# Attention and a mixture of experts on one core: the hand-written order of the attention's steps, all eight plans arranged anew

## Chip, cores and metric

One core of a Trainium2 chip runs the whole program. The metric is the device time of one execution in microseconds. The engines are named as in the profile: PE (TensorE), with PEld for its weight loads, ACT (ScalarE), DVE (VectorE), POOL (GpSimd) and SP (SyncE, which only issues DMAs here).

## What is computed

```python
def _attn_ref(q, k, v):                      # (8, 8, 576, 64), float32
    scores = scale * np.matmul(q, k.transpose(0, 1, 3, 2))
    mask = block_i >= block_j                # blocks of 64 positions
    scores = np.where(mask, scores, -1e9)
    scores = scores - np.max(scores, axis=-1, keepdims=True)
    attn = np.exp(scores)
    attn = attn / (np.sum(attn, axis=-1, keepdims=True) + 1e-09)
    return np.matmul(attn, v)
...
def _moe_ref(x, expert_emb, tau, w1, w2):    # x: 4608 rows of 512; 8 experts
    logits = xn @ en.T / tau                 # xn, en: rows divided by their norms
    expert_idx = np.argmax(logits, axis=1)
    gate_w = softmax(logits)[expert_idx]
    out[rows of e] = gate_w * (np.maximum(x @ w1[e], 0.0) @ w2[e])
```

## The kernel before

The 64 heads are worked off as 32 pairs (n = 0 to 31), four pairs to one of the 8 batches. Every pair goes through six kinds of work, each a Python generator that yields after every step. One letter of a plan string drives one generator by one step, so the string fixes the program order of all instructions, and with it the order in which each engine's queue gets them; each engine takes its queue strictly in order. In pair n the letters stand for:

- **s** (`scores`, 10 steps s1 to s10, five a head): scores of pair n, by a matmul over `ka`, `qb` (L400) and one over `kx`, `qx` (L401) into one of two PSUM tiles `pss`; then ACT takes the exp into `pT` (L410, L419), and POOL adds up `pT` into `pS` (L391).
- **v** (`values`, 9 steps): values of pair n-1. v1 to v6 multiply `pT` by `vo` (L435), where each head writes 64 columns of the array; v7 makes the sums over `pT` and `pS` with 32 columns each (L444, L445, L449); v8 is the copy of the result on ACT (L451); v9 is empty. All write the one PSUM tile `psb`.
- **f** (`post`, `finish`, 4 steps): pair n-1 is turned back. f1 and f2 are matmuls out of `so` into `psb` (L472, L476), f3 and f4 the divisions on DVE (L480 to L493).
- **m** (`maxes`, 12 steps): row maxima of pair n+1. m1 to m10 are a matmul into one of two PSUM tiles `psm` (L365) and a reduction on DVE (L367); m11 turns the maxima (L372), ACT copies them to `nmT` (L374), and two DMAs on SP's queue write them into a row of `qx` (L376), which the first score step of pair n+1 reads. m12 only ends the generator.
- **p** (`prep`, 6 steps): queries and keys of pair n+2. p1 transposes the queries on PE into the one PSUM tile `pst` (L322), ACT casts them (`qb`, L334); p2 casts `qd` (L338); p2 and p3 take the low parts on DVE (L311). p4 transposes the keys into `pst`, ACT casts `kd` (L343), SP issues four DMAs of `ka` (L346); p5 and p6 are the low parts.
- **r** (`slow[0]`): one step of the route of the batch before, if one is left: some 26 small DVE steps, a ranking on PE ("rk", L558 to L562), five squares and one exp on ACT, the store on SP, five scatters on POOL. The route of the seventh batch is followed by `early_rows`, which reads the table back by a DMA on SP (L649). An r without work does nothing.
- **w** and **l**: DMAs of `v` of pair n+3 on POOL's queue, and of `q`, `k` of pair n+3 on SP's.

```python
for c in PLANS[n % NP + (NP if n >= NPAIR - NP else 0)] if n else PLAN0:
    ...
    elif c != "r":
        parts[c] = drain(parts[c], 1)
    if c == "r" and slow and drain(slow[0], 1) is None:
        slow.pop(0)
```

Pair 0 has its own plan, plan n % 4 serves pairs 1 to 27 (plan 0 for six of them, plans 1 to 3 for seven each), and plans 4 to 7 the last four pairs. Pair 30 has no p left, pair 31 neither m nor p. After the pairs come the last values and finish, the slots' table, and the experts' layers (L1046), which the change doesn't touch.

Of the kernel before, what the change touches and what calls it, by code (L numbers as in the profile page):

```python
# [18 lines left out]


PLANS = (
    "rrrrlrvrvvvrvrrvrrrrsmmvvvmrrrmrrrrssprrrmrrrrrsrrmfprmmsrrrrrrrrsprrfrrmmsrsrmmffrrrrrrrrrprprrrsrprrrrrrrrswrrr",
    "vvvvrvvmmssvvmvmsspmsmpfmmsplfmsmspfmsmswfrpp",
    "mrmvvvrvvvvlrvmvpmssmwpfmrmsrpsfmrmssprmsfsrmfsrppms",
    "rrmmrvvlvvrvvvrrrvvmrmssrpwrmrssmpfmmrssfpmmfrssmpfsrrrmsrpprrr",
    "lvvvvmmpsrmsrrrrmvvpprrrvvrrrssrrrrvmmrppsrrsrrmrfrmrsrrpsrrrrmmffsfrmsrwm",
    "mrrmlpvvrvvrvprpvrmmrssrprmsmvsvrmvrsrrsmfmrrfrrrrmrfrswsmsmfrrprsrrrp",
    "prmmvvvrrvrvvrmssrpmrrrrrrrvvrsrmsmvrssrmmfmmfrrrsrlrfrsprprfwrprmrmsrps",
    "vvvmmrvmssvmmrvmmrpmrrssvsrvsmvrsrsrppmlfrfssmppmrfwpf",
)  # L30
PLAN0 = "kmsmsmmsmmkpsmsspkmmmpmslwsspspp"

# [1392 lines left out]
```

## Time and profile before

| | |
|---|---|
| median of three runs | 867.48 us (866.99 to 870.44) |
| profiled execution | 867.11 us |
| its span, first to last instruction | 865.4 us |
| mean granted clock of TensorE | 0.987 |
| busy: PE, PEld, DVE, ACT, POOL | 839.7, 676.4, 585.2, 491.4, 593.4 us |
| pairs 0 to 31 end at about | 410 us of the span |

Busy times are unions of the instructions' spans; matmuls are pipelined and overlap, so a busy PE need not be a PE at its peak. In the timelines below, rows stand in order of start, equal instructions that follow each other are merged with their count, and the distance between the starts of two rows is the time for which the first one kept PE from the second.

### The profile page before, as it was taken

The numbers are of one execution on the slowest core, as the hardware profiler recorded it, in microseconds if no ns is written. First come the engines' busy times: TensorE is split into PE (matmuls) and PEld (weight loads), VectorE is DVE, ScalarE is ACT, GpSimd is POOL, SyncE is SP. The second block draws the span as 40 slices with busy tenths as digits, with TensorE's granted clock in tenths as the row PEclk, the third lists the DMA queues.
The fourth block names the chain that finished last, engine by engine and source line by source line (L and its number), as shares of the span: only waits on it lengthen the run. The fifth ranks groups of instructions, "written<-read, shape, count | busy, mean of one in ns | idle before, by whom it ended". The sixth has DMA issues, their size and how long they took to land. (4 is left out here: it accounts for less than half of the span.)

```text
span 865.4 us, 19039 instructions
## 1 busy us (share of the span) xinstructions
PE 839.7 (97%) x5148; PEld 676.4 (78%) x5148; DVE 585.2 (68%) x1275; ACT 491.4 (57%) x959; POOL 593.4 (69%) x756
## 2 busy tenths in 40 slices
PE   8999999999999999998899999999999999999996
PEld 4777787777877788776678888888888888888874
DVE  8567887888888897883885634755766544665541
ACT  4556786868776776875745544654645333553321
POOL 6466787887778787688444444656677787777871
PEclk8799999999999999999999999999999999999998
DMA  7787887778788878884547434646777444444441
GB/s 151 175 186 145 173 179 171 167 167 174 168 182 173 171 178 177 191 202 148 160 128 276 142 133 148 220 166 209 237 247 238 156 154 149 140 144 148 152 121 34
DMA packets 141532, 146.69 MB, mean 170 GB/s; under 512 B 98889, under 2 KB 108329, under 8 KB 139852
## 3 DMA queue, kind: packets, MB, share of 16 engines
q1 hardware_dynamic: 115868, 91.58, 43.2%
q0 software_dynamic: 18896, 41.45, 16.6%
q10 hardware_dynamic: 6624, 12.06, 3.8%
q8 instruction: 51, 0.84, 0.4%
q14 instruction: 93, 0.76, 0.3%
HBM read 85.12 MB, written 31.79 MB: 135 GB/s over the span
## 5 line engine op out<-in xcount | busy, mean ns | idle before, releaser
L367 DVE TENSOR_REDUCE nmx<-psm 128x1 f32<-128x320 f32 x315 | 135.6, 453 | 54.0 <-PE psm L365 49.0
L410 ACT ACTIVATE pT<-pss 128x448 f32<-128x448 f32 (+1 forms) x254 | 108.1, 449 | 60.0 <-PE pss L401 57.7
L391 POOL TENSOR_TENSOR pS<-pS,pT 128x320 f32<-128x320 f32 x189 | 112.3, 594 | 17.4 <-ACT pT L410 2.7
L400 PE MATMUL pss<-qb,ka 128*128 128x448 f32 (+1 forms) x382 | 117.7, 322 | 3.4 <-ACT pT L410 1.4
L1046 PE MATMUL py<-ring_h,hh 128*128 (+1 forms) x288 | 112.7, 391 | 0.5 <-issue 0.5
L401 PE MATMUL pss<-qx,kx 70*128 70x448 f32 (+1 forms) x382 | 108.5, 311 | 4.9 <-DMA qx<-nmT 3.7
L1046 PE MATMUL py<-ring_h,hl 128*128 (+1 forms) x288 | 112.2, 390 | 0.0
L1046 PE MATMUL py<-ring_l,hh 128*128 (+1 forms) x288 | 112.1, 389 | 0.0
L391 POOL TENSOR_TENSOR pS<-pT 128x448 f32<-128x448 f32 x63 | 71.9, 1141 | 58.0 <-ACT pT L410 57.2
L1046 PE MATMUL ph<-ring_h,xh 128*128 x280 | 110.0, 393 | 0.0
L1046 PE MATMUL ph<-ring_h,xl 128*128 x280 | 109.3, 390 | 0.0
L1046 PE MATMUL ph<-ring_l,xh 128*128 x280 | 109.2, 390 | 0.0
L365 PE MATMUL psm<-kd,qd 128*128 128x320 f32 x315 | 98.3, 365 | 0.8 <-DVE nmx L367 0.4
L435 PE MATMUL psb<-pT,vo 128*64 128x448 f32 (+4 forms) x768 | 95.4, 397 | 1.2 <-issue 1.1
L812 DVE TENSOR_TENSOR ring_l<-raw,ring_h 128x1024 f32 (+1 forms) x64 | 83.0, 1308 | 19.1 <-ACT ring_h L808 14.3
L400 PEld LDWEIGHTS pss<-qb,ka 128*128 128x128 f32 x382 | 73.3, 192 | 18.2 <-ACT pT L410 11.1
L1064 ACT ACTIVATE h<-ph 128x512 f32<-128x512 f32 x70 | 41.7, 597 | 79.3 <-PE ph L1046 65.5
L435 PEld LDWEIGHTS psb<-pT,vo 128*64 128x64 f32 x768 | 50.6, 138 | 43.4 <-issue 32.8
L401 PEld LDWEIGHTS pss<-qx,kx 70*128 70x128 f32 x382 | 73.5, 193 | 7.3 <-DMA qx<-nmT 3.3
L973 POOL DMA_INDIRECT xg<-xbuf,rowq x64 | 64.9, 1014 | 20.4 <-issue 18.9
L973 POOL DMA_INDIRECT ex<-xbuf,rowq x64 | 63.4, 991 | 20.0 <-issue 17.1
L808 ACT CAST ring_h<-raw 128x1024 f32 (+1 forms) x68 | 70.3, 1053 | 6.8 <-ACTq L955 4.1
(278 smaller groups left out, 1815.5 us busy)
## 6 DMA issues: line engine op xcount, KB each, us to landing
raw<-in_moe_w_dram SPq DMA_DIRECT2D x40, 512.0 KB
ka<-kd SPq DMA_DIRECT2D x128, 144.0 KB
raw<-in_moe_w_dram SPq DMA_DIRECT2D x12, 1024.0 KB
hrows<-h ACTq DMA_DIRECT2D x46, 256.0 KB
hq<-hrows POOLq DMA_DIRECT2D x92, 128.0 KB, 3.1
qn<-in_q_dram SPq DMA_DIRECT2D x64, 144.0 KB
kn<-in_k_dram SPq DMA_DIRECT2D x64, 144.0 KB
qx<-qb SPq DMA_DIRECT2D x32, 288.0 KB
```

What stands on the lines that cost most here:

```text
L365: nc.tensor.matmul(mx[:, 0:max(e - a, 256)], qd[d][:, j, :, :], kd[d][:, a:a + max(e - a, 256)], start=True, stop=True)
L367: nc.vector.tensor_reduce(m[:, j + u:j + u + 1], mx[:, 0:e - a], axis=AX.X, op=ALU.max, negate=True)
L391: eng.tensor_tensor(o, pT[0:r, P:S] if t == 1 else o, pT[0:r, off[t]:off[t] + w], op=ALU.add)
L400: nc.tensor.matmul(o, ka[i][:, hh, ts], qb[i][:, hh, c0:c1], start=True, stop=False)
L401: nc.tensor.matmul(o, kx[i][0:KX, hh, ts], qx[i][0:KX, hh, c0:c1], start=False, stop=True)
L410: nc.scalar.activation(pT[:, o:o + c1 - c0], st[:, 0:c1 - c0], AF.Exp, scale=scale)
L435: nc.tensor.matmul(ob[hh * D:(hh + 1) * D, c0:c1], a[:, t, hh, :], pTs[hh][0][:, o:o + c1 - c0], start=(t == 0), stop=(c0 == OB or t == NJ ...
L808: return nc.scalar.copy(piece(ring_h, to, c, half), raw[i][:, c * CW:(c + 1) * CW])
L812: return eng.tensor_tensor(piece(ring_l, to, c, half), raw[i][:, c * CW:(c + 1) * CW], piece(ring_h, to, c, half).bitcast(F32), op=ALU.sub ...
L973: nc.gpsimd.indirect_dma_start(out=to, out_offset=None, in_=src, in_offset=bass.IndirectOffsetOnAxis(ap=at, axis=0))
L1046: m = nc.tensor.matmul(out, a[:, c, :], w, start=(c == 0 and w is wh and a is sh), stop=(c == nk - 1 and a is sl_))
L1064: nc.scalar.activation(h[:, f:f + 512], ph, AF.Relu)
```

## The change

The eight strings of `PLANS` are replaced; `PLAN0` and all else stay. The numbers of s, v, f, m and p steps are the same in each plan, r varies. In plans 0 to 3 v1 to v6 stand in two groups (with v7 apart from them: three) where they were one, and m steps often stand two together, between scores.

```diff
 PLANS = (
-    "rrrrlrvrvvvrvrrvrrrrsmmvvvmrrrmrrrrssprrrmrrrrrsrrmfprmmsrrrrrrrrsprrfrrmmsrsrmmffrrrrrrrrrprprrrsrprrrrrrrrswrrr",
-    "vvvvrvvmmssvvmvmsspmsmpfmmsplfmsmspfmsmswfrpp",
-    "mrmvvvrvvvvlrvmvpmssmwpfmrmsrpsfmrmssprmsfsrmfsrppms",
-    "rrmmrvvlvvrvvvrrrvvmrmssrpwrmrssmpfmmrssfpmmfrssmpfsrrrmsrpprrr",
-    "lvvvvmmpsrmsrrrrmvvpprrrvvrrrssrrrrvmmrppsrrsrrmrfrmrsrrpsrrrrmmffsfrmsrwm",
-    "mrrmlpvvrvvrvprpvrmmrssrprmsmvsvrmvrsrrsmfmrrfrrrrmrfrswsmsmfrrprsrrrp",
-    "prmmvvvrrvrvvrmssrpmrrrrrrrvvrsrmsmvrssrmmfmmfrrrsrlrfrsprprfwrprmrmsrps",
-    "vvvmmrvmssvmmrvmmrpmrrssvsrvsmvrsrsrppmlfrfssmppmrfwpf",
+    "vvrrvmrmprrrssmrmvvvmwrrrsrrmrsrlrrvrrmvsrrrsprrrrrmmrrprfmrffrrrsrfrsmprprrsrrrpmsvr",
+    "vrlvvvmssmmsmsrpmmrvrvvmmvsspmpfmfswsmfpfrpsvspm",
+    "vrvrvrvmsmpmsmvvvvswsplpmmfmffsspmmsfsmvrrrrrppsmmrs",
+    "rmrvrvrrrvvrmmpmvvrrmsrrsrvvmmsrlspmrrrfrrrrpmrrsrrrsrmrrrfssfmpsfpmrrrsvrrwp",
+    "rrmrmvvrrplrrrrmrsrrrrmvrvvrppvwvrvvmrsmrprrrmrsprrsrrmrprrfrrmrssrmfsfrrrmsrrfmsrsr",
+    "rrrmpmvvrsrlrrrsmrrrrpsvvvvrrrvrmrrrvrsmsmrrfpwmrsmrrpmrmrfssfmfmrpsrvrpsr",
+    "rmmvprrprrrlvrvrvrrvvvmvrsmsmrrpsprrsmmrfrprmsrmspmfrsffsmwrmsrsv",
+    "prvrvrmvrmvmmrmpssrvrvrrrmrrrssprvmvrlsrsrrsrrmmmrmrsrrrrfrpfrprfrrwsvpfrsm",
 )
 PLAN0 = "kmsmsmmsmmkpsmsspkmmmpmslwsspspp"
```

## Rows read from the trace of the kernel before

**Rows 1.** Profile page, part 1: busy time, share of the span, instructions.
```profile
PE 839.7 (97%) x5148; PEld 676.4 (78%) x5148; DVE 585.2 (68%) x1275; ACT 491.4 (57%) x959; POOL 593.4 (69%) x756
```

**Rows 2.** Stretches: length, busy (count) of PE, PEld, DVE, ACT, POOL; clock; DMA.
```profile
157.50:205.70 48.20, 47.76 (x396) 38.32 (x396) 40.47 (x116) 35.83 (x81) 38.22 (x51) 1.00 0.81 174
```

**Rows 3.** PE's timeline, plan 1: start, length, instruction, count.
```profile
177.49 0.28 PE L400 MATMUL pss<-qb,ka 128*128 128x256 f32 x1
177.61 0.29 PE L401 MATMUL pss<-qx,kx 70*128 70x256 f32 x1
...
177.97 2.92 PE L435 MATMUL psb<-pT,vo 128*64 128x128 f32 x24
180.82 0.53 PE L365 MATMUL psm<-kd,qd 128*128 128x320 f32 x2
181.19 0.30 PE L400 MATMUL pss<-qb,ka 128*128 128x288 f32 x1
```

**Rows 4.** PE's timeline, around score steps in plans 3 and 2.
```profile
162.83 0.66 PE L472 MATMUL psb<-idx,so 128*128 128x144 f32 x4
163.23 0.49 PE L365 MATMUL psm<-kd,qd 128*128 128x256 f32 x2
163.82 0.40 PE L400 MATMUL pss<-qb,ka 128*128 128x288 f32 x1
...
198.02 0.49 PE L365 MATMUL psm<-kd,qd 128*128 128x256 f32 x2
198.71 0.39 PE L400 MATMUL pss<-qb,ka 128*128 128x256 f32 x1 [0.20 <-ACT pT L410]
```

**Rows 5.** PE's timeline, three places in plans 2, 5 and 7.
```profile
146.21 0.29 PE L400 MATMUL pss<-qb,ka 128*128 128x288 f32 x1
147.17 0.40 PE L401 MATMUL pss<-qx,kx 70*128 70x288 f32 x1 [0.67 <-DMA qx<-nmT]
...
376.68 0.30 PE L401 MATMUL pss<-qx,kx 70*128 70x288 f32 x1
378.01 0.69 PE L322 MATMUL pst<-ident,kn 96*128 96x96 f32 x6 [1.03 <-issue]
...
400.52 0.40 PE L400 MATMUL pss<-qb,ka 128*128 128x288 f32 x1
402.26 0.40 PE L401 MATMUL pss<-qx,kx 70*128 70x288 f32 x1 [1.35 <-DMA qx<-nmT]
```

**Rows 6.** SP's timeline before the first and last of these places.
```profile
141.14 3.11 SPq L346 DMA_DIRECT2D ka<-kd  x4
144.35 1.56 SPq L376 DMA_DIRECT2D qx<-nmT  x2
...
399.98 0.34 SPq L649 DMA_DIRECT2D et<-table  x1
400.41 1.58 SPq L376 DMA_DIRECT2D qx<-nmT  x2
```

**Rows 7.** PE's timeline in plan 4, where the products stand in two groups.
```profile
358.75 2.48 PE L435 MATMUL psb<-pT,vo 128*64 128x128 f32 x16
361.16 0.53 PE L365 MATMUL psm<-kd,qd 128*128 128x320 f32 x2
...
363.56 0.37 PE L365 MATMUL psm<-kd,qd 128*128 128x448 f32 x1
363.86 0.66 PE L435 MATMUL psb<-pT,vo 128*64 128x192 f32 x8
364.45 0.30 PE L444 MATMUL psb<-pT,ones 128*32 128x128 f32 x1
```

**Rows 8.** ACT's groups by form, 157.5 to 205.7: busy, mean ns; idle before.
```profile
L338 ACT CAST qd<-qb 64x576 fp32r<-64x576 f32 x8 | 5.3, 666 | 0.1
```

**Rows 9.** DVE's timeline, first and last row of step f3, plan 3.
```profile
356.89 0.15 DVE L480 TENSOR_SCALAR rin<-psb 128x2 f32<-128x2 f32 x1
...
357.94 0.20 DVE L493 TENSOR_TENSOR lgh<-psb,rin 128x48 f32<-128x48 f32 x1
```

## The prediction

> **What bounds the kernel now.** I read the page first, then busy time by stretches, then the timeline of TensorE (PE) from start to start, and last the timelines of SP and VectorE (DVE) at the places where PE stood still. The page has PE busy 97% of the span [rows 1], but a matmul's row reaches past the start of the next one, so rows overlap and "busy" hides what a matmul costs. The distance between two starts is what counts below.
>
> The attention part repeats exactly every four pairs, since plans 0 to 3 take turns; I call that a round. A round takes 48.2 us, and in it DVE is busy 40.5 us, ScalarE (ACT) 35.8, GpSimd (POOL) 38.2 and PE 47.8, at a granted clock of 1.00 [rows 2]. So PE sets the pace, DVE has 16% to spare, and an order can win only what PE loses by waiting or by changing its mode.
>
> What one matmul takes: 0.12 us for 256 columns (177.49 to 177.61) [rows 3], so I price others by their columns, 0.21 us for 448, 0.27 us for 320 and 256 together, 0.13 us for 288.
>
> What PE waits for. (a) Score steps: two pss buffers, so step s waits for the exp of the second step before it. From 163.23 two matmuls of 256 (0.24 us) reach to 163.82: 0.35 us lost; from 198.02 the same work reaches to 198.71: 0.45 us lost [rows 4]. A round has four such places of 0.33 to 0.45 us and two or three smaller ones, 2.0 us together. (b) The first score step of a pair needs the maxima's row, brought by two DMAs on SP: at 146.21 PE goes on only at 147.17, 0.83 us late [rows 5]. SP had four ka transfers to issue first, 3.11 us from 141.14, and the nmT ones came behind them at 144.35 [rows 6]. That is at the first scores of plan 2, and plan 1 has p4 (which issues ka) before the maxima's last step m11. It occurs in three rounds, 2.6 us together. (c) In the last round: p4 waits from 376.68 to 378.01 for its one pst buffer, 1.2 us late, and the first score of the last pair from 400.52 to 402.26, 1.6 us late [rows 5], because SP sat in the route's table read (L649, at 399.98) before it could issue nmT at 400.41 [rows 6].
>
> **The change, part by part.** No instruction is added or removed: the same steps in another order on each queue.
>
> *Mode changes.* The values' products (v1 to v6) use 64-column tiles, their sums (v7) 32-column tiles, all else the whole array. Plans 0 to 3 had v1 to v6 in one stretch. That stretch takes 2.85 us (177.97 to 180.82), and the two matmuls behind it 0.37 us instead of 0.27, as the first load of weights lies open [rows 3]. Old plan 4 already splits them: v1 to v4 take 2.41 us and v5, v6 0.59 us, 0.15 us more than in one piece, and the matmul of 448 columns ahead of the second stretch holds PE 0.30 us instead of 0.21 [rows 7]. So one more visit to the tiles costs 0.15 + 0.09 + 0.10 = about 0.35 us, half of it for each change of mode. Counted from the strings (PE steps alone, r, w and l left out), the changes of mode rise by 2 in plan 0 (runs 6 times), 1 in plan 1, 2 in plan 2 and 3 in plan 3 (7 times each): 12 + 42 = 54. Plans 4 and 7 keep theirs, plan 5 has one more, plan 6 one fewer. 54 x 0.175 = **+9.5 us**. No cover hides it: PE is the engine that sets the pace. Below: if a change of mode falls into time in which PE would wait anyway, it costs nothing; above, 0.45 us a visit, 12 us.
>
> What the load behind a stretch shows is open time, 0.10 us. The Trainium skill's TensorE: Matmul & The Clock Gate (its opening table, queue depth) has TensorE pull weight loads ahead of matmuls in flight; by that the 0.10 would go and the sum would be 27 x 0.25 = 6.8 us. Its TensorEngine Tiling (Array Packing), Key Properties, says that changing the tiling mode drains the engine, which would leave 9.5 us. The trace sides with the second.
>
> *Score steps against ACT.* The casts of qd (two of 0.67 us [rows 8]) and the copy of so stand in ACT's queue near the middle of each pair, and the waits (a) lie behind them. Between s6 and s7, old plan 0 gives PE f2, m9, m10: 0.40 us for the four matmuls of f2 (162.83 to 163.23) [rows 4] and 0.24, so 0.64. The new one has m8, m9, f1, m10, f2 there: with f1 at some 0.8 (six such matmuls and three small transposes, by the same row) about 1.6. In plan 1 the work before s7 grows alike, in plan 2 that before s5 (m5, m6, f1, m7, f2 where f2, m8, m9 stood). Three of the four large waits should go, with the load left open behind each: about 1.1 us a round. In plan 3 only m10 and f2 stand between s6 and s7, so that one stays.
>
> *DVE's queue.* What comes in their place. (i) f3 and f4 free the one psb buffer that v1 of the next plan needs. f3 is DVE work from 356.89 to 358.14, 1.25 us [rows 9]. New plans 1 and 3 put f3 next to m11, and plans 2 and 0, which follow them, begin with v1; in the old order plan 2 began with two maxima, and plan 3 had f3 ahead of s7. (ii) New plan 3 has the route's exp (ACT) and the two steps that read it in the middle of the pair, next to each other, where the old order had p5 and p6 between: DVE then stands until ACT has got through the qd casts, and m9, m10, f3 and f4 wait behind it, on PE m11 and v1. Neither wait shows in the trace of before, so I bound the two: nothing, if DVE's 16% covers them, and at most ACT's two casts plus f3, 2.6 us a round. I take 0.8, nearer to the bottom, as the route's other work is as long as before. Net with the 1.1 above: -0.3 us a round, 6.75 rounds, **-2.0 us**; bounds -13 (all 2.0 us go, nothing comes) and +10.
>
> *SP's queue.* In new plans 0, 1 and 3 m11 stands ahead of p4, so nmT no longer queues behind ka; in plan 2 the next scores come 5 us later. PE has v1 to v4, m1 and more between m11 and the first score, about 4 us. Wait (b) goes: **-2.6 us** (bound 0, if the shorter way to s1 uncovers it elsewhere).
>
> *Last round.* The table read moves from behind f2 of plan 6 to before its s3, well ahead of m11, so SP is free for nmT: -1.6. p4 of plan 5 moves far behind p1: -1.2. But plan 5 has the route's ranking on PE (rk) directly behind m3, after eight DVE steps that begin with the plan; PE reaches it after about 2.8 us, DVE after 3 to 4: +0.8. **-2.0 us**; bounds -6 (all waits of these four pairs) and +2. The last pair has neither m nor p, and its order on PE is as before.
>
> GpSimd and the clock: plan 0's loads of v (w) now stand directly behind v6, which delays the adds of this pair, but the sums that need them come a pair later; PE stays busy, so I expect 1.00 throughout.
>
> Sum: 9.5 - 2.0 - 2.6 - 2.0 = +2.9 us. The profiled execution took 867.11 us, 0.4 below the median of 867.48 and 1.7 above its own span; 867.1 + 2.9 = **870.0 us**.
>
> **Rivals.**
> 1. The waits go and nothing takes their place (faster). For it: the stretches of v gave ACT nothing to do for 2.9 us at a time, and with scores between them ACT and DVE are fed evenly. The 1.4 us of mode changes a round also gives both more time. Against it: f3, f4 late in plans 1 and 3. Then -1.8 us a round, -12, with 9.5 - 2.6 - 3: **859 us**. It decides from about 1.7 us a round of waits removed.
> 2. DVE's queue takes over (slower): the exp of plan 3 and f4 before v1 hold PE 2.3 us a round where I took 0.8. Then 9.5 + 8 - 2.6 - 1: about **881 us**. For it: DVE is at 84% already. Against it: it idles at the start of most pairs. It decides from about 1.2 us a round.
> 3. The order does nothing: visits to the tiles fall where PE would wait anyway, and waits only change places: 867 us. It is part of "within 0.5%".
>
> **Numbers.** Differences under 0.5%, 4.3 us, can hardly be told from none here. The forecast with rival 3 gets 0.40, rival 1 0.26, rival 2 0.34. Faster is rival 1: 0.26; slower is rival 2 with the upper edge of the forecast, 0.38; within, 0.36. The range from 859 to 884 leaves out the far ends of both rivals.
>
> **What would show it.** A round in the new trace: 48.2 + 1.4 - 0.3 = about 49.3 us by the forecast, under 48 by rival 1, over 50.5 by rival 2. Two stretches of L435 a pair, three of L435 and L444 in plan 3, with 0.37 us behind each. No gap at the first L401 of plan 2 in the early rounds, nor near 402 us. By rival 2, L435 or L372 starts late behind DVE in plans 0, 2 and 3. The forecast is wrong if a visit costs much less than 0.35 us, or if ACT's waits return at other steps.

## The result and the profile after

The changed kernel takes 876.6 us (median of seven runs, 875.4 to 877.7), the kernel before 867.48 (seven runs beside them): a ratio of 1.0087, 95% interval 1.006 to 1.0115. The profiled execution is the slowest of the seven (877.7); it has a span of 876.0 us, 10.6 more than before, at a mean granted clock of 0.989.

Part 1 of the page, and a steady round of four pairs, cut from the last score of pair 16 to that of pair 20:

```profile
PE 846.6 (97%) x5148; PEld 672.1 (77%) x5148; DVE 603.6 (69%) x1275; ACT 489.0 (56%) x959; POOL 598.3 (68%) x756
```
```profile
230.73:280.56 49.83, 48.74 (x394) 37.64 (x392) 42.65 (x117) 35.30 (x80) 38.53 (x52) 1.00 0.76 169
```

The counts on the page are those of [rows 1]. The round takes 49.83 us where it took 48.2 [rows 2], at a clock of 1.00 in both. DVE is busy 2.2 us longer in it with the same work.

A pair's length is the distance between the starts of the last L401 of 64 columns of two successive pairs. In us, pairs 17 to 20, by the plan that orders them:

| kernel | plan 1 | plan 2 | plan 3 | plan 0 | four pairs |
|---|---|---|---|---|---|
| before | 11.82 | 12.68 | 11.75 | 11.93 | 48.18 |
| after | 12.28 | 12.62 | 12.88 | 12.05 | 49.83 |
| e1_split | 12.17 | 13.17 | 12.20 | 12.19 | 49.73 |
| e2_join | 11.96 | 12.32 | 12.90 | 12.70 | 49.88 |
| e5_route3 | 17.75 | 12.63 | 12.05 | 12.29 | 54.72 |
| e8_m11first | 12.01 | 12.75 | 11.77 | 11.92 | 48.45 |

Up to the end of pair 27 the new kernel is 9.8 us behind (368.3 against 358.5). The last four pairs give back 2.0 (417.8 against 410.0). From there to the end of the span it needs 2.8 more (458.2 against 455.4): 9.8 - 2.0 + 2.8 = 10.6. Two of these three hold a part that belongs to the execution and not to the order. In the last four pairs a stretch at half clock (0.50 granted) took 1.6 back (pair 29 below). And the 2.8 are 4.2 more in the seam, as I call the time from the last score to the 200th of the experts' products (70.1 against 65.9), and 1.4 less behind the last product (7.3 against 8.7), where executions with the old last strings differ as much: 7.0 in e3_new0to3, 9.4 in e6_et.

**Two visits to the tiles.** PE's timeline in pair 13 (plan 1):

```profile
180.66 2.48 PE L435 MATMUL psb<-pT,vo 128*64 128x128 f32 x16
183.07 0.42 PE L365 MATMUL psm<-kd,qd 128*128 128x320 f32 x1
183.33 0.29 PE L400 MATMUL pss<-qb,ka 128*128 128x288 f32 x1
...
186.78 0.41 PE L365 MATMUL psm<-kd,qd 128*128 128x320 f32 x1 [0.27 <-DVE nmx L367]
187.12 0.66 PE L435 MATMUL psb<-pT,vo 128*64 128x192 f32 x8
187.71 0.30 PE L444 MATMUL psb<-pT,ones 128*32 128x128 f32 x1
```

2.41 and 0.59 us are what plan 4 of the kernel before showed for the two groups [rows 7]. The maxima's matmul ahead of the second group waits for DVE.

**Who is waited for.** PE's loads of weights, waits by cause from 100 to 420 us; first the kernel before, then after:

```profile
PEld pss L400 <- ACT pT L410: 10.0, 30, 0.8
PEld psm L365 <- DVE nmx L367: 2.3, 7, 0.4
```
```profile
PEld pss L400 <- ACT pT L410: 2.8, 9, 0.4
PEld psm L372 <- DVE nmx L367: 6.2, 6, 1.0
PEld psm L365 <- DVE nmx L367: 5.2, 16, 0.5
```

The score waits of [rows 4] are mostly gone, and waits for the maxima have come: 7.2 us less of the one, 9.1 more of the other. The six at L372 are step m11 of plan 3, one a round. PE, DVE and ACT around the one in pair 19:

```profile
267.28 0.28 PE L372 MATMUL psm<-ident,nmx 128*9 128x128 f32 x1 [0.65 <-DVE nmx L367]
...
265.35 0.20 DVE L611 TENSOR_REDUCE gs<-lg 128x5 f32<-128x40 f32 x1 [0.84 <-ACT lg L609]
...
266.01 0.76 DVE L311 TENSOR_TENSOR qb<-pst,qb 64x576 fp32r<-64x576 f32 x1
266.80 0.42 DVE L367 TENSOR_REDUCE nmx<-psm 128x1 f32<-128x128 f32 x2
...
263.70 1.36 ACT L338 CAST qd<-qb 64x576 fp32r<-64x576 f32 x2
265.08 0.24 ACT L609 ACTIVATE lg<-lg 128x40 f32<-128x40 f32 x1
```

ACT comes to the route's exp (L609) behind its two qd casts, DVE stands 0.84 us in front of L611, and behind L611 in its queue are two more route steps, p3's low part and the last two maxima. Those end past 267, and m11 with them.

**Pair 29** got longer (15.98 us against 14.69), and that is the clock of this execution. In it the granted clock is at 0.50, its lower level (1.2 GHz), for 3.4 us; before had none between 33.6 us and the kernel's last 6. e9_lock_after and e2_join have the same strings for the last four pairs and ran pair 29 at full clock; and with the strings of before pair 29 met the lower level too, in e1_split and e8_m11first:

| execution | strings of the last four pairs | at half clock in pair 29 | pair 29 | the four pairs |
|---|---|---|---|---|
| before | old | none | 14.69 | 51.5 |
| e9_lock_after, e2_join | new | none | 14.36, 14.37 | 47.9, 47.9 |
| e1_split, e8_m11first | old | 3.4 us | 16.19, 16.09 | 52.9, 52.9 |
| after | new | 3.4 us | 15.98 | 49.5 |

So at like clock the new strings win 3.4 to 3.5 us in the four pairs, and pair 29 is 0.1 to 0.3 us shorter. It is so although the ranking waits for DVE (1.06 us here, 0.78 in e9), and a small comparison of DVE takes six times its usual 0.20 us, for as long as POOL's addition beside it runs. PE, DVE and POOL after, then the stretch at half clock, and the whole pair in e9 (columns as in [rows 2]):

```profile
385.53 0.18 PE L558 MATMUL psm<-ohb,triS 128*128 128x40 bf16 x1 [1.06 <-DVE ohb L550]
384.12 1.23 DVE L548 TENSOR_TENSOR ohb<-t,mx 128x40 bf16<-128x40 f32 x1
384.17 1.13 POOL L391 TENSOR_TENSOR pS<-pT 128x448 f32<-128x448 f32 x1
```
```profile
385.80:389.20 3.40, 3.40 (x11) 1.28 (x12) 2.02 (x7) 2.08 (x6) 2.49 (x4) 0.50 0.99 324
```
```profile
379.57:393.93 14.36, 13.16 (x106) 9.71 (x105) 12.70 (x42) 11.13 (x28) 10.49 (x16) 1.00 0.74 204
```

**Pair 31** is 2.2 us shorter. Its first scores run without the wait of [rows 5], since SP had issued nmT by 399.1:

```profile
397.56 1.55 SPq L376 DMA_DIRECT2D qx<-nmT  x2
...
401.20 0.30 PE L400 MATMUL pss<-qb,ka 128*128 128x288 f32 x1
401.33 0.30 PE L401 MATMUL pss<-qx,kx 70*128 70x288 f32 x1
```

**Behind the pairs** DVE splits the experts' first weights (L812) and turns the low part of their inputs (`xl`, L1039), on which PE waits. Ahead of that it makes four of the last pair's additions (L391). DVE and POOL in the kernel before:

```profile
411.23 1.00 DVE L391 TENSOR_TENSOR pS<-pT 128x448 f32<-128x448 f32 x1
413.93 2.36 DVE L812 TENSOR_TENSOR ring_l<-raw,ring_h 128x1024 fp32r<-128x1024 f32 x2 [0.18 <-ACT xh L1038]
416.21 0.68 DVE L1039 TENSOR_TENSOR xl<-pe,xh 128x512 fp32r<-128x512 f32 x1
416.81 7.31 DVE L812 TENSOR_TENSOR ring_l<-raw,ring_h 128x1024 fp32r<-128x1024 f32 x3
...
415.88 2.69 POOL L812 TENSOR_TENSOR ring_l<-raw,ring_h 128x1024 fp32r<-128x1024 f32 x1 [2.67 <-ACT ring_h L808]
420.24 6.11 POOL L812 TENSOR_TENSOR ring_l<-raw,ring_h 128x1024 fp32r<-128x1024 f32 x2 [1.67 <-ACT ring_h L808]
```

and after, with PE's two waits:

```profile
419.07 1.95 DVE L391 TENSOR_TENSOR pS<-pT 128x448 f32<-128x448 f32 x1
423.27 4.53 DVE L812 TENSOR_TENSOR ring_l<-raw,ring_h 128x1024 fp32r<-128x1024 f32 x2 [0.25 <-issue]
427.72 0.68 DVE L1039 TENSOR_TENSOR xl<-pe,xh 128x512 fp32r<-128x512 f32 x1
428.32 7.81 DVE L812 TENSOR_TENSOR ring_l<-raw,ring_h 128x1024 fp32r<-128x1024 f32 x3
...
423.71 3.01 POOL L812 TENSOR_TENSOR ring_l<-raw,ring_h 128x1024 fp32r<-128x1024 f32 x1 [0.77 <-ACT ring_h L808]
...
428.46 0.50 PE L1046 MATMUL pss<-ring_h,xl 128*128 128x512 f32 x1 [3.23 <-DVE xl L1039]
437.25 0.50 PE L1046 MATMUL pss<-ring_h,xl 128*128 128x512 f32 x1 [1.47 <-DVE xl L1039]
```

POOL's piece begins 5.9 us behind the last score in both kernels. DVE comes later: POOL's gathers and additions of the last pair end 5.1 us behind that score (3.2 before), DVE's four additions beside them take 3.7 us (2.3 before), and its first subtraction starts 1.5 us later. Its first two subtractions then take 4.53 us instead of 2.36: before, POOL's piece began when they were nearly done; now POOL begins 0.44 us behind DVE's start, and DVE's second one waits it out. In the kernel before only the second of PE's waits is there, 0.92 us. In e2_join, with the same last strings, POOL's piece came 0.8 us later, DVE's two took 2.36, and the seam is 67.4 us, 1.5 over before's.

### The profile page after: what moved, and what is told of

Read it like the earlier page. It is cut to its first block, busy times and chain, and to the rows that moved or that the text cites. A ratio compares the mean times of both kernels' runs of the same rounds, so it can differ in the third digit from the quotient of the medians.

```text
span 876.0 us, 19023 instructions
## 1 busy us (share of the span) xinstructions
PE 846.6 (97%) x5148; PEld 672.1 (77%) x5148; DVE 603.6 (69%) x1275; ACT 489.0 (56%) x959; POOL 598.3 (68%) x756
## 5 line engine op out<-in xcount | busy, mean ns | idle before, releaser
L410 ACT ACTIVATE pT<-pss 128x448 f32<-128x448 f32 (+1 forms) x254 | 109.2, 451 | 68.6 <-PE pss L401 61.7
L391 POOL TENSOR_TENSOR pS<-pS,pT 128x320 f32<-128x320 f32 x189 | 112.6, 596 | 23.6 <-ACT pT L410 6.6
L391 POOL TENSOR_TENSOR pS<-pT 128x448 f32<-128x448 f32 x63 | 72.4, 1150 | 68.8 <-ACT pT L410 68.6
L400 PE MATMUL pss<-qb,ka 128*128 128x448 f32 (+1 forms) x382 | 118.2, 325 | 0.5 <-ACT pT L419 0.4
L401 PE MATMUL pss<-qx,kx 70*128 70x448 f32 (+1 forms) x382 | 108.4, 310 | 3.1 <-DMA qx<-nmT 2.9
L365 PE MATMUL psm<-kd,qd 128*128 128x320 f32 x315 | 104.3, 365 | 2.2 <-DVE nmx L367 1.9
L435 PE MATMUL psb<-pT,vo 128*64 128x448 f32 (+4 forms) x768 | 103.2, 405 | 1.8 <-issue 1.1
L812 DVE TENSOR_TENSOR ring_l<-raw,ring_h 128x1024 f32 (+1 forms) x64 | 85.6, 1349 | 19.1 <-ACT ring_h L808 13.9
L435 PEld LDWEIGHTS psb<-pT,vo 128*64 128x64 f32 x768 | 48.7, 139 | 42.7 <-issue 36.9
L365 PEld LDWEIGHTS psm<-kd,qd 128*128 128x128 f32 x315 | 56.4, 191 | 31.7 <-issue 17.8
L400 PEld LDWEIGHTS pss<-qb,ka 128*128 128x128 f32 x382 | 73.6, 193 | 8.5 <-ACT pT L410 3.4
L401 PEld LDWEIGHTS pss<-qx,kx 70*128 70x128 f32 x382 | 73.7, 193 | 5.1 <-DMA table<-zcol 2.6
```

Of the source, the lines that this page charges most:

```text
L365: nc.tensor.matmul(mx[:, 0:max(e - a, 256)], qd[d][:, j, :, :], kd[d][:, a:a + max(e - a, 256)], start=True, stop=True)
L391: eng.tensor_tensor(o, pT[0:r, P:S] if t == 1 else o, pT[0:r, off[t]:off[t] + w], op=ALU.add)
L400: nc.tensor.matmul(o, ka[i][:, hh, ts], qb[i][:, hh, c0:c1], start=True, stop=False)
L401: nc.tensor.matmul(o, kx[i][0:KX, hh, ts], qx[i][0:KX, hh, c0:c1], start=False, stop=True)
L410: nc.scalar.activation(pT[:, o:o + c1 - c0], st[:, 0:c1 - c0], AF.Exp, scale=scale)
L435: nc.tensor.matmul(ob[hh * D:(hh + 1) * D, c0:c1], a[:, t, hh, :], pTs[hh][0][:, o:o + c1 - c0], start=(t == 0), stop=(c0 == OB or t == NJ ...
```

## The experiments

All were timed beside the kernel before: e1 to e4, e5 to e8 and e9 to e12 went together, with medians of 867.2, 866.9 and 869.5 for it. Ratios are to it, with 95% intervals.

### e1_split: the second visit to the tiles alone

The plans of before, with one PE step (s or m) moved between v4 and v5 in plans 0 to 3, so that the changes of mode rise by 54:

```diff
-    "vvvvrvvmmssvvmvmsspmsmpfmmsplfmsmspfmsmswfrpp",
+    "vvvvrmvvmssvvmvmsspmsmpfmmsplfmsmspfmsmswfrpp",
...
-    "rrmmrvvlvvrvvvrrrvvmrmssrpwrmrssmpfmmrssfpmmfrssmpfsrrrmsrpprrr",
+    "rrmmrvvlvvrmvvvrrrvvrmssrpwrmrssmpfmmrssfpmmfrssmpfsrrrmsrpprrr",
```

> The order of before; in plans 0 to 3 alone, v5 and v6 move behind the next score or maxima step, so that every pair of these plans visits the 64-column tiles twice (54 changes of mode more, as many as the change adds). Theory A, each change of mode costs PE 0.175 us: +9.5 us, about 877 us, and a round of 49.6 us where before has 48.2. Rival B, the visits fall into time in which PE would wait anyway: within 2 us of before.

876.8 us, ratio 1.0104 (1.0065 to 1.0143). The four pairs of the table grow by 0.35, 0.49, 0.45 and 0.26: 1.55 us for four added visits, 0.39 each, with whatever else the moved step did. This edit alone makes the kernel as slow as the whole change.

### e2_join: the change without the second visit

The new plans with v1 to v6 in one stretch in plans 0 to 3 (40 changes of mode fewer):

```diff
-    "vrlvvvmssmmsmsrpmmrvrvvmmvsspmpfmfswsmfpfrpsvspm",
+    "vrlvvvvvmssmmsmsrpmmrrvmmvsspmpfmfswsmfpfrpsvspm",
...
-    "rmrvrvrrrvvrmmpmvvrrmsrrsrvvmmsrlspmrrrfrrrrpmrrsrrrsrmrrrfssfmpsfpmrrrsvrrwp",
+    "rmrvrvrrrvvvvrmmpmrrmsrrsrvvmmsrlspmrrrfrrrrpmrrsrrrsrmrrrfssfmpsfpmrrrsvrrwp",
```

> The changed order; in plans 0 to 3 alone, v1 to v6 are put back together at the place of the first group (40 changes of mode fewer). Theory A: 40 x 0.175 = 7.0 us under the changed kernel, about 869.5 us. Rival B, the changed order loses by DVE's queue and not by its tiles: it stays within 2 us of 876.6, and the waits of m11 and of the maxima remain.

877.0 us, ratio 1.0112 (1.0074 to 1.015): nothing won. Plans 1 and 2 gain 0.3 each, plan 0 loses 0.65. Pair 20, DVE and PE:

```profile
271.55 0.82 DVE L367 TENSOR_REDUCE nmx<-psm 128x1 f32<-128x320 f32 x2 [1.92 <-PE psm L365]
...
268.25 2.92 PE L435 MATMUL psb<-pT,vo 128*64 128x128 f32 x24
273.71 0.44 PE L365 MATMUL psm<-kd,qd 128*128 128x384 f32 x1 [0.58 <-DVE nmx L367]
```

DVE has nothing to do for 1.92 us during the one stretch, and right behind it PE waits for DVE, as the maxima come two at a time. Within this order the second visit pays for itself; that it does so by feeding DVE in between is read from these rows.

### e3_new0to3 and e4_new4to7: either half of the change

e3 has the new strings for plans 0 to 3 and the old ones for 4 to 7, e4 the reverse:

```diff
-    "vvvvrvvmmssvvmvmsspmsmpfmmsplfmsmspfmsmswfrpp",
+    "vrlvvvmssmmsmsrpmmrvrvvmmvsspmpfmfswsmfpfrpsvspm",
...
-    "vvvmmrvmssvmmrvmmrpmrrssvsrvsmvrsrsrppmlfrfssmppmrfwpf",
+    "prvrvrmvrmvmmrmpssrvrvrrrmrrrssprvmvrlsrsrrsrrmmmrmrsrrrrfrpfrprfrrwsvpfrsm",
```

> New plans 0 to 3, old plans 4 to 7. If the rounds cost what the end of pair 27 shows in the changed kernel (9.8 us later than before) and the last four pairs and the tail are as before: 877.3 us. If the changed kernel's 2.8 us in the tail come from the new rounds and not from the new last plans: about 880 us.

> Old plans 0 to 3, new plans 4 to 7. Theory: the last four pairs win 2.0 us on PE, and the tail gives 2.8 us back since GpSimd's gathers and adds no longer end before DVE's late work: 868.3 us, the last score step about 2 us earlier than before and the first expert matmul behind its longest wait about 1 us later. Rival, the tail's loss has another cause: 865.5 us.

e3: 876.0 us, 1.0095 (1.0058 to 1.0132), near the 877.3 of the first theory; behind by 9.3 us at the end of pair 27, and its tail is 454.0 us long, no longer than before's. e4: 870.6 us, 1.0033 (1.0005 to 1.0061), more than either theory has; no loss up to pair 27, and the tail 458.2, as the first one has it. But the last four pairs took 51.8 us against 51.5, with 3.4 us at half clock in pair 29, and 14.57 in pair 28, where the new plan 4 stands behind an old plan 3 (12.51 in the change). So the rounds lose by plans 0 to 3, and the longer seam comes with plans 4 to 7 (66.0 us in e3, 70.0 in e4).

### e5_route3: the route's steps behind m11

```diff
-    "rmrvrvrrrvvrmmpmvvrrmsrrsrvvmmsrlspmrrrfrrrrpmrrsrrrsrmrrrfssfmpsfpmrrrsvrrwp",
+    "rmrvrvrrrvvrmmpmvvrrmsrrsrvvmmsrlspmrfpmssmfssfmpsfprrrrmrrrsvrrrrrrrrrrrrrwp",
```

> All eight new plans; in plan 3 only, the route's steps gs, gs+, rcp2, its store and scatters stand behind f4 and p5 instead of ahead of m8 and m11 (the exp stays where it is). Theory A, that VectorE stands behind the exp of the route and m11 is late for that (0.83 us each on the path, about 0.1 of load besides, in seven rounds): about 6 us go, 870.5. Theory B, that VectorE is simply behind with the maxima in twos, whatever stands ahead of m11: m11 waits as before, the time stays at 876 (875 to 877).

889.6 us, ratio 1.0256 (1.022 to 1.0291): neither theory has that. At the place itself the first one holds: m11 has no wait, and plan 3's pair falls by 0.83, from 12.88 to 12.05, of which plan 0's pair behind it gives 0.24 back. What was lost is in plan 1's pair: 3.3 to 5.5 us more in pairs 9, 13, 17, 21 and 25. The route's store went along with the steps, to a later place in SP's queue. PE (the m11 of pair 11, the scores of pair 13) and SP of e5:

```profile
167.15 0.27 PE L372 MATMUL psm<-ident,nmx 128*9 128x128 f32 x1
186.23 0.61 PE L401 MATMUL pss<-qx,kx 70*128 70x288 f32 x1 [2.45 <-DMA qx<-nmT]
...
173.57 1.17 SPq L512 DMA_DIRECT2D gbuf<-xrow  x1
174.79 0.85 SPq L513 DMA_DIRECT2D gbuf<-xrow  x1
175.74 1.02 SPq L211 DMA_DIRECT2D qn<-in_q_dram  x2
```

In the changed kernel SP issues these two at 166.1 and 166.7 and comes to qn at 171.98; here the store's four DMAs stand between ka and qn, and q, k and the transfers behind them start 3.5 us later. The hardware queue from 177 to 184 us, in the changed kernel and in e5 (packets, MB, share of 16 engines):

```profile
q1 hardware_dynamic: 565, 0.53, 45.9%
```
```profile
q1 hardware_dynamic: 3059, 1.03, 87.2%
```

The nmT transfers are issued at the same place in the pair (180.32 against 180.13) and are 2.45 us late for the score; that the fuller queue is what held them is argued from these two rows. After that the granted clock is at half for 3.4 to 6.8 us in each of these five pairs, which is part of the loss. (These rows are of an execution of 895.8 us.)

### e6_et: the table's read behind the maxima's loads

Plans of before; in plan 6 the table's read stands behind m11:

```diff
-    "prmmvvvrrvrvvrmssrpmrrrrrrrvvrsrmsmvrssrmmfmmfrrrsrlrfrsprprfwrprmrmsrps",
+    "prmmvvvrrvrvvrmssrpmrrrrrrrvvrsrmsmvrssrmmfmmfslfsppfwpmmrrrrrrrsrrrrprs",
```

> All eight old plans; in plan 6 the table's read and the steps of the route behind it stand later, behind m11 and s, so that the 16-bit loads of the next pair's maxima are not queued behind it on SyncE. Theory A, that the 1.6 us wait at the first score of pair 31 is worth its length to the end: 865.6. Theory B, that the tail (VectorE and POOL at the same additions, the gathers that come no earlier) gives it back: pair 31 about 1.6 us shorter, the part behind it longer by as much, 867.2.

869.3 us, ratio 1.0044 (1.0015 to 1.0073). Pair 31 is 1.5 us shorter (10.62 against 12.10), as foreseen, and the tail 2.5 longer (457.9 against 455.4): 1.1 of it in the seam, where DVE's first subtraction starts 1.1 us later than before, behind additions that ran beside POOL's as in the change; 0.7 between the 200th and the last product and 0.8 behind it, where the other executions differ by 0.5 and by 2.4 among themselves. In the profiled executions the won time is given back (865.6 against 865.4), and by the ratio somewhat more.

### e7_rk: the ranking later

Plan 5 of the change with rk behind v6 and v7:

```diff
-    "rrrmpmvvrsrlrrrsmrrrrpsvvvvrrrvrmrrrvrsmsmrrfpwmrsmrrpmrmrfssfmfmrpsrvrpsr",
+    "rrrmpmvvrsrlrrrsmpsvvvvvrrrrmvsmrrrrsmrrrrfpwmrrsmrpmrmrfssfmfmrpsrvrpsr",
```

> All eight new plans; in plan 5 the route's ranking product and the additions behind it stand later, behind v7 and the spread of the other steps, so that TensorE does not come to it ahead of VectorE's one-hots. Theory A, that the wait of 1.1 us there and the drop of the granted clock that follows are what makes pair 29 longer than before: 2 to 3 us go, about 874, and no stretch of half clock stands in pair 29. Theory B, that pair 29 is long for the crowd of steps on VectorE and ScalarE and the clock falls on its own: under 1 us, 875.5 to 876.5.

876.4 us, ratio 1.0102 (1.0074 to 1.013), not the 874 of theory A. The ranking starts without a wait and no half clock stands in pair 29, yet the pair takes 15.92 us (15.98 in the profiled execution of the change). This does not show that the clock cost nothing before: the same pair without this edit takes 14.36 us at full clock (e9), so the edit itself costs 1.6 us. PE's rows show a wait for the maxima, and there are longer waits for the exps besides:

```profile
385.60 0.19 PE L558 MATMUL psm<-ohb,triS 128*128 128x40 bf16 x1
...
387.27 0.44 PE L365 MATMUL psm<-kd,qd 128*128 128x384 f32 x1 [0.77 <-DVE nmx L367]
```

Theory A's question is settled by e9: at full clock pair 29 of the changed strings isn't longer than before's, the wait for the ranking and all.

### e8_m11first: nmT ahead of ka alone

Plans of before; in plan 1 one swap:

```diff
-    "vvvvrvvmmssvvmvmsspmsmpfmmsplfmsmspfmsmswfrpp",
+    "vvvvrvvmmssvvmvmsspmsmpfmmsplfmsmsmfpsmswfrpp",
```

> All eight old plans; in plan 1 the step m11 stands ahead of p4 instead of behind it, so that the loads of the next pair's maxima are issued ahead of the keys' transfers. Theory A, that the score waits for these loads in the early rounds (0.9 us in three rounds) go and nothing takes their place: about 864.7. Theory B, that m11 then waits on VectorE for the last maxima, or the keys come later and the score waits for them instead: 867.2.

868.2 us, ratio 1.0009 (0.9983 to 1.0036). The wait of [rows 5] at 146.21 is gone (from 130 to 190 us before has 1.0 us there, e8 none), and m11 waits 0.4 for DVE instead: 0.2 to 0.3 us a round in all the other rounds. Theory B. The waits were worth less than their length, too: before's pairs 2, 6 and 10 take 13.38, 12.78 and 13.12 us, where its later pairs of plan 2 take 12.7, 1.2 us over them in all.

### e9 to e12: POOL's three subtractions on VectorE

```diff
-        split_lo(0, c, 0, eng=nc.gpsimd if c == NPC - 1 else nc.vector)
+        split_lo(0, c, 0, eng=nc.vector)
...
-        split_lo(1, c, 1, to=0, eng=nc.vector if c < 2 else nc.gpsimd)
+        split_lo(1, c, 1, to=0, eng=nc.vector)
```

e9 is the changed kernel with this edit, e10 the kernel before with it, e11 adds it to e4 and e12 to e6.

> The kernel after the change, with its eight plans; behind the last pair, the three subtractions of the first weights that POOL makes (2.7 to 3.1 us each in its row) go to VectorE (1.2 us each), the same sums otherwise. Theory A, that the tail is 2.8 us longer because VectorE's own two subtractions (4.53 us for two, where before had 2.36) stand still while POOL's runs: the first wait of the experts' products goes from 3.4 to about 1.2 us and the second from 1.6 to about 1.1, 873 to 874. Theory B, that VectorE is simply the bound there and each subtraction given to it costs 1.2 us more: 876.5 to 880.

> The kernel before the change, with the same three subtractions moved from POOL to VectorE. Theory A: VectorE's first two were clear of POOL's there (2.36 us for two), but the next three took 7.31 us while POOL ran two; six on VectorE alone would take about 7.2, so the second wait of the experts' products stays (0.9 us) and the pieces that POOL finished late come 2 us earlier: 866 to 867.5. Theory B: each costs 1.2 us more on the path, 868.5 to 871.

> Old plans 0 to 3, new plans 4 to 7 (870.55 by itself, with a tail 2.8 us longer than before), and the three subtractions on VectorE. Theory A (VectorE stands still while POOL works): the tail's 2 to 2.5 us come back, 867.5 to 868.5. Theory B: 870.5 or more.

> All old plans with the table's read behind the maxima's loads in plan 6 (pair 31 1.5 us shorter, the tail up to the first experts' products about 1 us longer, 869.3 measured against 866.9), and the three subtractions on VectorE. Theory A: VectorE's first two take 2.4 us and the third does not hold POOL's place, the experts' waits fall from 3.4 us in sum to about 2.2, and pair 31's gain shows: 865.5 to 866.5. Theory B: 869 or more.

e9: 873.4 us, 1.0037 (1.001 to 1.0065), where the change alone has 876.6 and 1.0087; the kernel before had 869.5 us in this group and 867.5 beside the change, so the ratios overstate the gain. DVE and PE:

```profile
420.40 2.36 DVE L812 TENSOR_TENSOR ring_l<-raw,ring_h 128x1024 fp32r<-128x1024 f32 x2 [0.25 <-issue]
422.68 0.69 DVE L1039 TENSOR_TENSOR xl<-pe,xh 128x512 fp32r<-128x512 f32 x1
423.28 6.89 DVE L812 TENSOR_TENSOR ring_l<-raw,ring_h 128x1024 fp32r<-128x1024 f32 x6
...
423.42 0.50 PE L1046 MATMUL pss<-ring_h,xl 128*128 128x512 f32 x1 [1.09 <-DVE xl L1039]
431.29 0.50 PE L1046 MATMUL pss<-ring_h,xl 128*128 128x512 f32 x1 [0.54 <-DVE xl L1039]
```

Six subtractions on DVE alone (6.89 us) take less than three of them beside two of POOL's (7.81), the first two are back at 2.36, and the seam falls from 70.1 to 68.0 us. Theory A. (Of the 5.2 us by which the profiled spans differ, 1.6 are pair 29's clock.) e11: 867.7, 0.9982 (0.9951 to 1.0013), as theory A has it; its seam is 2.1 us shorter than e4's (67.9 against 70.0). e10: 868.4 us, 0.9981 (0.9946 to 1.0016), between the theories; its seam is 0.65 longer than before's (66.55 against 65.90), since DVE's first two were free there already. e12: 867.3, 0.9981 (0.9952 to 1.0011), over the 866.5 of theory A; its seam is 0.65 longer than e6's (67.61 against 66.96). So e12's ratio, where e6 had 1.0044, is not shown to be the edit's doing, as the kernel before took 869.5 us in the one group and 866.9 in the other. e11 and e12 were meant as versions that beat both kernels. They beat the changed kernel, but none of e10 to e12 can be told from the kernel before.

## Why the prediction came out as it did

The forecast was 870.0 us, the kernel takes 876.6, inside the range from 859 to 884. The sign of the sum was right, its size a third of the measured 9.1 (2.9). The largest term held; the two terms of the rounds that should have paid for half of it were mis-sized, the last round won more than was taken, and the tail had no term.

- **Mode changes, +9.5.** Held, in the order of before. e1 prices a visit at 0.39 us against the 0.35 taken: 54 changes come to 10.5, and e1's ratio gives 0.0104 x 867 = 9.0. The rival that visits fall where PE waits anyway is out there. In the new order the price can't be had back by joining them: e2 has 40 changes fewer and the same time, as waits for DVE take their place. Behind the stretch in pair 13 the load shows again: 0.26 us from L365 to L400, where 320 columns cost 0.15. By the queue-depth rule of the Trainium skill's TensorE: Matmul & The Clock Gate (opening table) it would have gone; this row shows it once more.
- **Steady waits, -0.3 a round.** Both halves were too small. A round grew by 1.65 where the mode changes alone make 1.55 (e1), so the waits net about +0.1, if the two prices add up. ACT's score waits fell by more than the 1.1 a round (7.2 us over some six and a half rounds in L410's row alone, and more in L419's), and DVE's grew by more than the 0.8: 0.83 at m11 (e5 gives that back in plan 3's pair) and a third to half a microsecond at other maxima. The mechanism (ii), DVE standing behind exp and casts, was right, its place too; (i), v1 waiting for f3 and f4, shows in no row.
- **nmT behind ka, -2.6.** Mostly not won. e8 makes this edit alone, and what three rounds win the others lose at m11, 0.2 to 0.3 each. The step "wait (b) goes" held but for 0.4 us at 47.9 and 0.2 at 146.2; that nothing came in its place did not, and the three waits were worth 1.2 us of pair length, not 2.6. With the row above: 9.8 us at the end of pair 27 against 9.5 - 2.0 - 2.6 = 4.9.
- **Last round, -2.0.** Measured -2.0 in the profiled execution, and that the figures meet is luck: the clock was expected at 1.00 throughout, and it fell in pair 29 for 3.4 us. At like clock it is -3.5: pair 31 -2.2 (forecast -1.6), pair 28 -0.6 and pair 30 -0.4 (neither was forecast), and pair 29 -0.3 (e9), where +0.8 for rk and -1.2 for p4 were taken, -0.4 together.
- **The tail.** The sum had no term for what is behind the pairs. The seam there costs +4.2: 1.5 as DVE's last additions run beside POOL's, 2.2 at DVE's second subtraction (3.39 us against 1.22), and the rest at PE's second wait; e9 takes 2.1 of it back. "GpSimd" was dismissed in a sentence, since its adds are wanted only a pair later. In the last pair its gathers and adds end 5.1 us behind the pair (3.2 before), when DVE's work is next.

The rest: a round takes 49.83 us, where the forecast had 49.3 and rival 2 over 50.5. Rival 2 had the right engine, at 2.3 us a round too dear; rival 1's waits went, but were replaced.

What remains open: how much the visits cost within the new order; why plan 1's pair takes 12.7 us in some rounds and 12.3 in others (which ones differs between executions of the same strings: pair 13 took 12.72 here and 12.26 in e7, pair 21 12.31 here and 12.72 in e9), why the granted clock falls in pair 29 in some executions and not in others, and what the clock does at the start of the kernel, where the profiled executions differ by some 3 us.

## What to carry to other kernels

When an order feeds a second engine more evenly, count what stands behind each of its waits before counting the gain: here the score waits went and the maxima's came, and the changes of mode stayed as the price. A step moved in a program takes its DMAs along, and one store moved behind the wrong transfer cost 3.3 to 5.5 us in each of five rounds. Before a longer stretch is put down to the order, look up its granted clock, and the same strings in another execution: pair 29 seemed 1.3 us longer and was 0.3 shorter. Add a term for the seam behind the loop, as engines that finish later there can run into each other.

## What the runs showed of the hardware

DVE stands still while POOL works, for some operations. One small step of the route, 128 by 40, in a round of the kernel before and in one after (columns: count, busy us, mean ns):

```profile
L544 DVE SCALAR_TENSOR_TENSOR t<-lg,erev 128x40 f32<-128x40 f32 x1 | 0.2, 199 | 0.0
```
```profile
L544 DVE SCALAR_TENSOR_TENSOR t<-lg,erev 128x40 f32<-128x40 f32 x1 | 1.6, 1558 | 0.0
L311 DVE TENSOR_TENSOR qb<-pst,qb 64x576 fp32r<-64x576 f32 x8 | 6.0, 755 | 0.2
```

L544, L541 (194 to 1086 ns) and L812 read two operands from SBUF and stretch, with POOL's L391 and L812 running; L311 and L1039, which read one operand from PSUM, keep their 0.75 and 0.68 us; in the kernel before L1039 took 0.67 at 424.51, amid POOL's 6.11. The Trainium skill's page SBUF — State Buffer, section Who interferes with whom, says that a VectorE instruction with two SBUF inputs contends with a GpSimd one that reads SBUF, and that the later one blocks until the first is done. The traces agree: L548 in pair 29 comes while POOL is at one addition (383.88 to 384.20) and ends within 0.05 us of the next (385.35 and 385.30), so it sat out both, whose spans touch, and e9's two L812 are back at 2.36 us without POOL. L544 and L541 alone add 2.2 us to DVE's time in a round, as much as it grew by; smaller ones went up and down.
